# Reordering the first two tiles of a retention-plus-MLP kernel: the second tile's first product ahead of the first tile's second one

## The chip, the cores and the metric

One core of a Trainium2 chip runs the whole program. The metric is the time of one execution on the device in microseconds (us). Engines are named as in the profile: PE is TensorE (PEld its weight loads), DVE is VectorE, ACT is ScalarE, POOL is GpSimd, SP is SyncE, which here issues DMAs only. A line number such as L662 is one of the kernel before, unless it is said to be of the kernel after.

## The reference

```python
def _attn_ref(q, k, v):                      # q, k, v: (8, 8, 576, 64) float32
    scores = np.matmul(q, k.transpose(0, 1, 3, 2)) / np.sqrt(D_)
    gamma = 1.0 - 2.0 ** (-5.0 - np.arange(H))
    rel = pos[:, None] - pos[None, :]
    Dmat = np.where(rel >= 0, gamma[:, None, None] ** rel[None, :, :], 0.0)
    return np.matmul(scores * Dmat[None], v)

def _moe_ref(x, w_in, w_out):                # x: (4608, 512), w_in: (512, 2048), w_out: (2048, 512)
    h = x @ w_in
    g = h * np.tanh(np.log1p(np.exp(h)))     # mish (h itself above 20)
    return g @ w_out
```

The attention's output, with heads side by side, is x. Inputs and output are float32; the kernel multiplies in bf16 and sums in float32.

## The kernel before, in words

**Tiles and chunks.** The 4608 rows of x are worked on as 9 tiles of 512 rows, each of 4 chunks of 128 rows. Tiles 0 and 1 hold the first 128 positions of batches 0 to 3 and 4 to 7; they need no earlier state, and have code of their own (the functions f_*). Chunks 8 to 35 follow: for each, q, k and v are loaded (`load`, by DMAs that POOL issues), multiplied by decay factors (`step_p`, L341, two instructions on DVE; `step_v`, L348, on DVE for chunks below 16, on POOL later), q and k are turned (`step_t`), and then scores (L382), states (L428, summed on DVE at L452), masks (`step_m`, L388) and outputs (L484, L500) follow in a "visit" of two chunks.

**First product of a tile.** `g1(t, f)`: for each of 16 blocks f of d_ff, four products of 128 x 128 weights w_in with 512 columns of x (L570; with `halved` set, the middle ones as two of 256 columns at L575), then Mish on ACT into gT (L586).

**Second product of a tile.** Tile 0: `g2_first`, plain, 4 row blocks x 16 products of 512 columns, with the result copied (L619) and stored. Tiles from 1 on: seven products of halves in place of eight (Strassen-Winograd's kind of scheme): w_out and g are each cut into 2 x 2 quarters; sums of quarters are made ahead (`w_sum`, L643, for w_out, once for all tiles; `g_sum`, L653, for g, five for each tile; each 128 x 2048 bf16), and `unit(t, k)` does half of one of the seven products, 8 matmuls of 256 columns at L662 (`seven`). `taken` moves each finished bank out of PSUM and combines the results; some of the additions are put off (`behind_visit`, `rest`).

**Order.** The scheduler is off: each engine runs its instructions in the order in which the program emits them, and waits on semaphores. The order is written out by hand. In the kernel before: g1(0, 0..15); then the 16 parts of g2_first with tile 1's preparation between them (T: turning, S: scores, V: casts of v, O: outputs, F: states); then the loop over u = 0..23, whose slots 0 to 15 are g1(1, u) and 16 to 23 are unit(1, 0..7), with the work of chunks 8 to 13 between them (`ps`, `vs`, `ts_` say at which u a chunk's P, V and T come). Then tiles from 2 on.

**Loads on POOL's queue.** All loads but the first two go through POOL. Its DMAs use eight semaphores in turn, so that an issue waits until the eighth one before it has landed, and POOL's other instructions stand in the same line. The order before: tile 0's q, k, v; w_in in five pieces; half of tile 1's q and k (L107); w_out 0 and 1 (L89); the other half of q and k; w_out 2 and 3; tile 1's v in two pairs (L118); mask (L935 to L938); chunks 8, 9 and on (L325). Chunks 10 to 17 wait, by a one-column copy on POOL (`landed`, L313), until v of the chunk two before has landed. Five buffers hold q and k of chunks (`qkraw`), seven hold v.

**Banks.** PSUM has the pools sc (2 x 2 banks), st (1), hp (2) and ops (1). Outputs of chunks 8 and 9 take ops and hp at u = 16.

Of the kernel before, what the change touches and what calls it, by code (L numbers as in the profile page):

```python
# [9 lines left out]
F32 = mybir.dt.float32  # L10
# [6 lines left out]
def kernel(  # L17
# [84 lines left out]
    def load_first_qk(t, i, b):  # L102

        name = ("qb", "kb")[i]
        if t not in fst:
            fst[t] = {"qb": stage[:, 0:4, :], "kb": stage[:, 4:8, :], "vb": {}}
        nc.gpsimd.dma_start(out=fst[t][name][:, b, :],  # L107
                            in_=(q, k)[i][4 * t + b, :, 0:P, :].rearrange("h (g r) d -> g h (r d)", r=8))
# [51 lines left out]

    def keep_warm(n, pool=ps_o, name="ops"):
        idle = pool.tile([P, 512], F32, name=name)
        for _ in range(n):
            nc.tensor.matmul(idle, lhsT=zeros[:, 0:P], rhs=zeros, start=True, stop=True)

# [55 lines left out]
    def f_v(t, b, copy):  # L221
# [5 lines left out]
        fst[t]["vb"][b] = vb  # L227

    def f_out(t, b, copy):
        if b == 0:  # L230
            xts[t] = xp.tile([P, KC, NCH * P], BF16, name="xT")
        vb = fst[t]["vb"][b]
        if t == 0:
            pool, name = ((ps_h, "hp"), (ps_h, "hp"), (ps_st, "st"), (ps_o, "ops"))[b]
            ot = pool.tile([P, NP, P], F32, name=name)
        else:
            if b % 2 == 0:
                fst[1]["out"] = ps_sc.tile([P, 2, NP, P], F32, name="sc")
            ot = fst[1]["out"][:, b % 2]
        for p in range(NP):  # L240
            for e in range(2):
                nc.tensor.matmul(ot[ds(64 * e, 64), p, :], lhsT=vb[:, 2 * p + e, :],
                                 rhs=fst[t]["sm", b][:, 2 * p + e, :],
                                 start=(p == 0), stop=True, skip_group_check=True)
        if t == 0:

            n = NP if b < 2 else NP // 2
            for p in range(0, NP, n):
                copy(xts[t][:, ds(p, n), ts(b, P)], ot[:, ds(p, n), :])
        elif b % 2:  # L250
            copy(xts[1].rearrange("p h (b i) -> p b h i", i=P)[:, ds(b - 1, 2)], fst[1]["out"])

# [309 lines left out]

    outs = {}
    halved = [0]
# [23 lines left out]

    def g2_first(part, s):

        if part == 0:
            pool, name = ((ps_h, "hp"), (ps_h, "hp"), (ps_o, "ops"), (ps_st, "st"))[s]
            outs[0, s] = pool.tile([P, d_model], F32, name=name)
        for f in range(4 * part, 4 * part + 4):
            halved[0] = int(f < 9)
            product(outs[0, s], gts[0][:, f, ts(s, P)], w_out_t[:, f, :], f == 0, f == nF - 1)
        if part == 3:
            store(0, s, outs[0, s], nc.scalar.copy if s % 2 else nc.vector.tensor_copy)

# [7 lines left out]
    def send(t, s):  # L607
# [4 lines left out]
        else:  # L612
            for e in range(2):
                nc.sync.dma_start(out=out[ds((b + e) * S + 512, 64), :], in_=ot[ds(64 * e, 64), :])

    def store(t, s, ops, copy):
        if s % 2 == 0:
            rows_of(t, s // 2)
        copy(rows[t, s // 2][:, s % 2, :], ops)  # L619
        send(t, s)  # L620

# [16 lines left out]
    def w_sum(i, engine=nc.vector):  # L638
        a, b, op_, to = {1: ((0, 0), (1, 1), OP.add, room[0]), 6: ((0, 0), (0, 1), OP.add, room[1]),
                         7: ((1, 0), (1, 1), OP.add, room[2]), 3: ((0, 1), (1, 1), OP.subtract, None),  # L640
                         4: ((1, 0), (0, 0), OP.subtract, room[6])}[i]
        to = w_half(*a) if to is None else to.rearrange("p (f d) -> p f d", f=hF)
        engine.tensor_tensor(to, w_half(*a), w_half(*b), op=op_)  # L643
        wsum[i] = to

    def g_sum(t, i, engine=nc.vector, to=None):
        a, b, op_ = {1: ((0, 0), (1, 1), OP.add), 2: ((1, 0), (1, 1), OP.add), 5: ((0, 0), (0, 1), OP.add),
                     6: ((1, 0), (0, 0), OP.subtract), 7: ((1, 1), (0, 1), OP.subtract)}[i]
        if to is None:
            to = room[3 + gsum.setdefault("n", 0) % 3]  # L650
            gsum["n"] += 1
# [25 lines left out]
    def taken(t, i, bank):  # L677

        tt = nc.vector.tensor_tensor
        in_rows = nc.gpsimd.tensor_tensor if t == nT - 2 else tt  # L680
        if i == 4 and t < NS:
            rows_of(t, 1)
            act(quarter(t, 1, 0), bank)
        elif i == 4:
# [4 lines left out]
        elif i == 1:  # L689
            if t >= NS:  # L690
                rows_of(t, 1)
            if (t, 0) not in rows:
                rows_of(t, 0)
            lower = fourth[t] if t >= NS else quarter(t, 1, 0)
            act(keep[1], bank)
# [24 lines left out]

    ORDER = {NS - 1: (4, 3, 2, 1, 6, 5, 7)}
    LIKE = {6: 3, 7: 5}
    banks = {}

    def unit(t, k):

        i, half = ORDER.get(t, (4, 2, 1, 3, 6, 5, 7))[k // 2], k % 2
        if half == 0 and i not in LIKE:
            beside = {4: (ps_h, "hp"), 3: (ps_st, "st")} if t < NS else \
                {2: (ps_st, "st"), 3: (ps_st, "st")} if t == nT - 2 else {}  # L730
# [106 lines left out]
    def tail(t):  # L837
# [21 lines left out]
        act(quarter(t, 0, 1), third)  # L859
        g_sum(t, 6, to=room[6])  # L860
        second = whole(2, ps_h, "hp")
# [35 lines left out]
    for b in range(2):  # L897
        dve(fst[0]["qb"][:, b, :], q0[:, b, :])
    keep_warm(12)
    f_transpose(0, 0, 1, [(ps_h, "hp", act), (ps_h, "hp", dve)])  # L900
    f_transpose(0, 0, 0, [(ps_st, "st", act), (ps_o, "ops", dve)])
    keep_warm(2, ps_sc, "sc")
    f_transpose(0, 1, 1, [(ps_h, "hp", act), (ps_h, "hp", act)])
# [3 lines left out]
    f_v(0, 1, act)  # L907
    load_w_in(1024, 512)
    keep_warm(3, ps_h, "hp")
    f_scores(0, 1)  # L910
    keep_warm(3)
    f_out(0, 0, act)
# [3 lines left out]
    f_v(0, 3, (act, pool))  # L916
    load_w_in(1536, 512)
    f_out(0, 2, act)
    f_out(0, 3, dve)
    keep_warm(2, ps_sc, "sc")  # L920
    f_k0_copy(0, turned, (dve, dve))
    for i, b in ((1, 0), (1, 1), (0, 0), (0, 1)):
        load_first_qk(1, i, b)
    for i in range(2):
        load_w_out(i)
        f_state(0, i)
    for i, b in ((1, 2), (1, 3), (0, 2), (0, 3)):
        load_first_qk(1, i, b)
    for b in (2, 3):
        f_state(0, b)  # L930
    for i in (2, 3):
        load_w_out(i)
    for b in (4, 6):
        load_first_v(b)
    nc.gpsimd.memset(mask, 1.0)  # L935
    for j in range(2):
        half = mask[ds(64 * j, 64)]
        nc.gpsimd.affine_select(out=half, in_=half, compare_op=OP.is_ge, fill=0.0,  # L938
                                base=0, pattern=[[1, 64]], channel_multiplier=-1)
    for b in range(4):  # L940
        load(N0 + b)
    nc.vector.tensor_scalar(gq, gq, 1.0 / math.sqrt(D), None, op0=OP.mult)


    for f in range(nF):
        halved[0] = 2
        g1(0, f)
    for i in range(2):
        f_mix(0, i)
    steps = {0: "T0", 3: "S0 C1", 9: "T1", 11: "S1", 12: "V0 V1 V2 V3", 14: "O0 O1 O2 O3", 15: "F0 F1"}  # L950
    for i in range(nF):
        for step in steps.get(i, "").split():
            n = int(step[1])
            if step[0] == "T":
                for j in range(2):
                    f_transpose(1, n, j, [(ps_sc, "sc", (dve, act)[j])])
            elif step[0] == "S":
                f_scores(1, n)
            elif step[0] == "V":
                f_v(1, n, dve if n == 3 else act)  # L960
            elif step[0] == "C":
                for j in range(2):
                    f_mix(n, j)
            elif step[0] == "F":
                f_state(1, n, nc.vector)
            else:
                f_out(1, n, (dve, act)[n // 2])
        g2_first(i // 4, i % 4)

# [11 lines left out]
    ts_ = {4: 0, 7: 1, 12: 2, 14: 3, 19: 4, 21: 5}  # L981
    FIRST = {1: (0, 0), 2: (1, 0), 3: ("turn", 1), 5: (0, 1), 6: (1, 1)}
    for u in range(24):
        j, w = divmod(u, 4)
        halved[0] = 2 if u < 1 else 0
        if u in FIRST:
            what, of = FIRST[u]
            if what == "turn":
                f_k0_copy(of, f_k0(of), (dve, act))
            else:  # L990
                first_states(of, what)
                if what:
                    first_states_copy(of, act)
        if u in ps:
# [3 lines left out]
        if u in vs:  # L998
            att(N0 + vs[u], "V")
        if u in (1, 2):  # L1000
            f_state(1, u + 1, nc.vector)
        for what in {7: "W4", 9: "W6 W3 W1", 19: "S1", 21: "S6"}.get(u, "").split():
            w_sum(int(what[1])) if what[0] == "W" else g_sum(1, int(what[1]))
        if w == 0 and j > 0:
# [23 lines left out]
        if u < nF:  # L1028
            g1(1, u)
            flush()  # L1030
# [17 lines left out]
    for t in range(NS, nT - 1):  # L1048
        for i in range(nF):
# [8 lines left out]
            if (t, i) in HALVED:  # L1058
                halved[0] = HALVED[t, i]
            for job in PLAN[i] if t > NS else {5: ("S5",), 8: ("W7",), 9: ("S7",)}.get(i, ()):  # L1060
                if job[0] == "S":
# [107 lines left out]
```

## Time and profile before

| | |
|---|---|
| median of 3 runs | 288.64 us (288.28 to 288.77) |
| the profiled execution | 288.53 us |
| its span, first to last instruction | 286.8 us |
| busy: PE, DVE, POOL, ACT | 276.7, 215.5, 172.0, 162.1 us |
| PE busy in 0 to 17 us, 17 to 49 us, 49 to 78 us | 13.28, 31.79, 28.42 us |
| DVE busy in the same stretches | 10.39, 14.50, 28.17 us |
| g1(0, 0) starts, tile 0's second product starts | 16.89 us, 31.67 us |
| g1(1, 0), slot u = 0, starts | 48.90 us |
| unit(1, 6), slot u = 22, starts | 77.20 us |

The page lists busy time by engine, the span in 40 slices, DMA queues, the chain that ended last, and groups of instructions by line. A timeline line has start, duration, engine, line, operation, output <- inputs, size, count, and in brackets how long the engine was idle before it and what ended that. The window table has, for each stretch, its length and the busy time of PE, PEld, DVE, ACT and POOL with numbers of instructions, then the granted PE clock (1.00 throughout), the DMA share and GB/s. The chain is followed back from the end; its lines have start, duration and what it was.

### The profile page before, as it was taken

What the parts mean: (1) busy time and instruction counts of PE and PEld (TensorE: products, weight loads), DVE (VectorE), ACT (ScalarE), POOL (GpSimd) and SP (SyncE); (2) the same over time, 40 slices, a digit from 0 to 9 for tenths busy, and PEclk for the clock granted to TensorE, in tenths of its full rate; (3) what the DMA queues carried; (4) which work ended last, traced back from release to release, by engine and by line L of the source; (5) the groups of instructions that cost most, each with busy time, mean ns of one, the idle gap of its engine ahead of it and who ended that gap; (6) DMA issues with size and microseconds to landing.
All of it is one profiled execution on the core that took longest, in us unless ns stands there. A gap on an engine that the chain in (4) does not pass through costs nothing.

```text
span 286.8 us, 8923 instructions
## 1 busy us (share of the span) xinstructions
PE 276.7 (96%) x3818; PEld 192.9 (67%) x3854; DVE 215.5 (75%) x302; ACT 162.1 (57%) x286; POOL 172.0 (60%) x243
## 2 busy tenths in 40 slices
PE   7799999999999999999999999999999999999994
PEld 3466775556876667666766666667666766888783
DVE  4740459999999996896599757974899194777783
ACT  5566415777776564565465555564566556476620
POOL 8686861687793999697929682969240000469500
PEclk9999999999999999999999999999999999999999
DMA  7999999978799994979599999697968001200323
GB/s 150 205 204 205 204 238 220 305 186 210 190 215 197 166 279 122 210 189 233 145 153 209 141 209 204 167 206 189 154 101 146 2 3 73 75 1 3 108 92 94
DMA packets 41545, 45.94 MB, mean 160 GB/s; under 512 B 23841, under 2 KB 31265, under 8 KB 41505
## 3 DMA queue, kind: packets, MB, share of 16 engines
q0 software_dynamic: 14256, 30.15, 50.1%
q1 hardware_dynamic: 26656, 14.69, 26.4%
q8 instruction: 30, 0.49, 0.8%
q10 hardware_dynamic: 592, 0.52, 0.6%
q14 instruction: 11, 0.08, 0.1%
HBM read 36.70 MB, written 9.44 MB: 161 GB/s over the span
## 4 chain that ended last, share of the span: by engine, by line
PE 69%; DMA 15%; DVE 7%; POOL 5%; issue 2%; ACT 1%; POOLq 0%; ACTq 0%; DVEq 0%
PE hp L570 28%; PE ops L662 27%; DMA w_out_t<-in_moe_w_out_dram 4%; DMA vraw<-in_v_dram 4%; DMA w_in_t<-in_moe_w_in_dram 4%; PE st L662 2%; DMA qkraw<-in_k_dram 2%; PE hp L662 2%; PE hp L778 2%; DVE qks L341 2%; PE sc L778 1%; PE sc L428 1%; PE sc L382 1%; PE sc L849 1%; POOL gT L107 1%
## 5 line engine op out<-in xcount | busy, mean ns | idle before, releaser
L570 PE MATMUL hp<-xT,w_in_t 128*128 128x512 bf16 x439 | 111.8, 379 | 1.8 <-issue 0.3
L586 ACT ACTIVATE gT<-hp 128x512 bf16<-128x512 f32 x129 | 76.9, 600 | 46.6 <-PE hp L570 42.2
L570 PEld LDWEIGHTS <-w_in_t 128*128 128x128 bf16 x474 | 45.3, 98 | 41.0 <-issue 0.9
L662 PEld LDWEIGHTS <-room 128*128 128x128 bf16 x608 | 58.8, 98 | 13.9 <-DVE room L653 0.3
L341 DVE TENSOR_TENSOR qks<-qkraw,gqk 128x512 bf16<-128x512 f32 x56 | 48.1, 908 | 10.1 <-issue 5.1
L653 DVE TENSOR_TENSOR room<-gT 128x2048 bf16<-128x2048 bf16 x40 | 50.8, 1289 | 1.1 <-ACT gT L586 1.1
L1045 POOL COPY held<-gT 128x1 bf16<-128x1 bf16 x58 | 23.0, 397 | 32.9 <-ACT gT L586 32.9
L662 PE MATMUL ops<-room,room 128*128 128x256 bf16 x320 | 40.1, 273 | 0.3 <-DVE room L653 0.2
L796 POOL TENSOR_TENSOR vraw<-vraw 128x256 f32<-128x256 f32 x7 | 6.5, 924 | 37.9 <-ACT vraw L790 37.8
L662 PEld LDWEIGHTS <-gT 128*128 128x128 bf16 x256 | 24.5, 98 | 6.2 <-ACT gT L586 0.4
L388 DVE TENSOR_TENSOR sm<-sc,mask 128x1024 bf16<-128x1024 f32 x14 | 17.1, 1218 | 11.7 <-PE sc L382 11.1
L348 POOL TENSOR_TENSOR vs<-vraw,gv 128x512 bf16<-128x512 f32 x20 | 25.5, 1297 | 0.0
L662 PE MATMUL ops<-w_out_t,room 128*128 128x256 bf16 x208 | 25.3, 273 | 0.0
L325 POOL DMA_DIRECT2D vraw<-in_v_dram x24 | 21.3, 886 | 2.5 <-DMA w_out_t<-in_moe_w_out_dram 1.4
L325 POOL DMA_DIRECT2D qkraw<-in_q_dram x24 | 21.7, 904 | 1.5 <-issue 1.2
L325 POOL DMA_DIRECT2D qkraw<-in_k_dram x24 | 21.2, 884 | 0.0
L452 DVE TENSOR_TENSOR total<-sc,total 128x256 f32<-128x256 f32 x32 | 13.5, 422 | 2.2 <-PE sc L428 1.4
L512 ACT CAST xT<-hp 128x512 bf16<-128x512 f32 x19 | 10.3, 589 | 7.6 <-PE hp L500 7.6
L662 PE MATMUL ops<-room,gT 128*128 128x256 bf16 x112 | 13.7, 272 | 0.2 <-ACT gT L586 0.2
L575 PE MATMUL hp<-xT,w_in_t 128*128 128x256 bf16 x92 | 13.8, 273 | 0.0
L575 PEld LDWEIGHTS <-w_in_t 128*128 128x128 bf16 x92 | 9.0, 98 | 5.4
L175 DVE COPY room<-gT 128x1024 bf16<-128x1024 bf16 x4 | 3.2, 828 | 9.7 <-DMA gT<-in_q_dram 9.7
(186 smaller groups left out, 423.6 us busy)
## 6 DMA issues: line engine op xcount, KB each, us to landing
out_dram<-res SPq DMA_DIRECT2D x29, 256.0 KB, 4.8
qkraw<-in_q_dram POOLq DMA_DIRECT2D x24, 256.0 KB, 6.1
qkraw<-in_k_dram POOLq DMA_DIRECT2D x24, 256.0 KB, 6.4
vraw<-in_v_dram POOLq DMA_DIRECT2D x24, 256.0 KB, 5.4
w_out_t<-in_moe_w_out_dram POOLq DMA_DIRECT2D x4, 512.0 KB, 11.3
w_in_t<-in_moe_w_in_dram POOLq DMA_DIRECT2D x3, 512.0 KB, 10.1
out_dram<-res SPq DMA_DIRECT2D x9, 128.0 KB, 2.4
gT<-in_k_dram POOLq DMA_DIRECT2D x8, 128.0 KB, 6.9
```

The source lines that it names most:

```text
L325: nc.gpsimd.dma_start(out=t, in_=src[b, :, ds(P * c, P), :].rearrange("h p d -> p h d"))
L341: nc.vector.tensor_tensor(slots[:, :, y], heads[:, :, y], factors[:, :, y].unsqueeze(3).to_broadcast([P, NP, 2, D]), op=OP.mult)
L348: engine.tensor_tensor(vs, live[n]["v"], gv[:, c, :].unsqueeze(2).to_broadcast([P, H, D]), op=OP.mult)
L388: nc.vector.tensor_tensor(sm.rearrange("p e x n i -> p (e x n) i"), live[n]["sc"].rearrange("p e x n i -> p (e x n) i"), mask.unsqueeze(1) ...
L452: nc.vector.tensor_tensor(new[:, k], st[:, j, x], total[b], op=OP.add)
L512: copy(xts[t][:, :, ds(P * s, 2 * P)].rearrange("p h (x j i) -> p j h x i", x=2, j=2)[:, j], both[j])
L570: nc.tensor.matmul(to, lhsT=w, rhs=x, start=first, stop=last)
L575: nc.tensor.matmul(to[:, ts(j, n)], lhsT=w, rhs=x[:, ts(j, n)], start=False, stop=False, skip_group_check=True)
L586: nc.scalar.activation(gts[t][:, f, :], hp, AX.Mish)
L653: engine.tensor_tensor(to, g_half(t, *a), g_half(t, *b), op=op_)
L662: nc.tensor.matmul(bank[:, half, :], lhsT=g[:, f, ts(half, P)], rhs=w[:, f, :], start=(f == 0 and half == 0 and not add), stop=(f == hF - ...
L1045: nc.gpsimd.tensor_copy(held[:, i % 2:i % 2 + 1], gts[t][:, f, 0:1])
```

## The change

1. After g1(0, f), which now has tile 1's first turning, scores and outputs (batches 4 and 5) between its last blocks, comes tile 1's first product, by halves of its batches: `g1_half(i, 0)` for batches 4 and 5, then `g1_half(i, 1)` for 6 and 7, each for two blocks of d_ff, 8 matmuls of 256 columns and one Mish. x of tile 1 is laid out as two halves (`x1`), and each half is copied by ACT and DVE together.
2. Tile 0's second product comes after that, by seven products of halves as in the other tiles, `unit(0, u - 2)` in the slots u = 2 to 15 that held g1(1, u). Its order is 5, 2, 7, 4, 3, 1, 6, and `taken_first` takes its banks. Its g sums 5 and 7 go to two of the five qkraw buffers (`ahead`); sums 2, 1 and 6 to room as in other tiles. `g2_first` and `store` are gone.
3. w_out's sums are all made ahead of tile 0's second product: 4, 6, 3 and 1 on DVE, and 7 on POOL. In the kernel before all are on DVE, 4, 6, 3 and 1 between u = 7 and 9, and 7 in tile 2.
4. Loads: half of tile 1's q and k goes ahead of the last three (smaller) pieces of w_in, then v, q and k of tile 1, and w_out last: pieces 2 and 3, then 0 and 1. Tile 1's q and k go to two of the buffers for output rows (`res`).
5. `f_state(0, b)` goes from POOL to DVE, `f_state(1, b)` from DVE to POOL, and tile 1's four casts of v go from ACT (three) and DVE (one) to POOL. w_sum 7 and the mask stand on POOL behind chunks 8 and 9's loads and ahead of chunk 10's.
6. The warming products on PE are cut into more and smaller ones.

Its core, with other parts left out:

```diff
@@ load_first_qk
-        if t not in fst:
-            fst[t] = {"qb": stage[:, 0:4, :], "kb": stage[:, 4:8, :], "vb": {}}
+        if t == 0 and t not in fst:
+            fst[0] = {"qb": stage[:, 0:4, :], "kb": stage[:, 4:8, :], "vb": {}}
+        elif t not in fst:
+            held_ = [op.tile([P, 2, d_model], F32, name="res").rearrange("p x d -> p (x d)").bitcast(BF16)
+                     for _ in range(2)]
...
@@ g2_first
+    def g1_half(i, j):
+
+        if 1 not in gts:
+            gts[1] = gp.tile([P, nF, NCH * P], BF16, name="gT")
+        hp = ps_h.tile([P, 2, 2 * P], F32, name="hp")
+        for a in range(2):
+            for c in range(KC):
+                nc.tensor.matmul(hp[:, a], lhsT=w_in_t[:, c, ts(2 * i + a, P)], rhs=x1[j][:, c, :],
+                                 start=(a == 0 and c == 0), stop=(c == KC - 1), skip_group_check=True)
+        nc.scalar.activation(gts[1][:, ds(2 * i, 2), ds(2 * P * j, 2 * P)], hp, AX.Mish)
...
+    def taken_first(i, bank):
+
+        tt, in_rows = nc.vector.tensor_tensor, nc.gpsimd.tensor_tensor
+        if i == 5:
+            rows_of(0, 0)
+            act(quarter(0, 0, 1), bank)
+        elif i == 2:
+            act(keep[0], bank)
+        elif i == 7:
+            act(quarter(0, 0, 0), bank)
+        elif i == 4:
+            lower = op.tile([P, 2, hD], F32, name="fourth", bufs=1)
+            act(lower, bank)
+            rows_of(0, 1)
+            behind_visit.append(lambda: in_rows(quarter(0, 0, 0), lower, quarter(0, 0, 0), op=OP.subtract))
+            behind_visit.append(lambda: in_rows(quarter(0, 1, 0), lower, keep[0], op=OP.add))
+        elif i == 3:
+            tt(quarter(0, 0, 1), bank, quarter(0, 0, 1), op=OP.add)
+        elif i == 1:
+            tt(quarter(0, 0, 0), bank, quarter(0, 0, 0), op=OP.add)
+            tt(quarter(0, 1, 1), bank, keep[0], op=OP.subtract)
+        else:
+            tt(quarter(0, 1, 1), bank, quarter(0, 1, 1), op=OP.add)
+
+    ORDER = {0: (5, 2, 7, 4, 3, 1, 6), NS - 1: (4, 3, 2, 1, 6, 5, 7)}
...
@@ the order, from the first loads on
-    keep_warm(12)
+    keep_warm(50, cols=122)
...
-    load_w_in(1024, 512)
-    keep_warm(3, ps_h, "hp")
+    load_w_in(1024, 256)
+    keep_warm(8, ps_h, "hp", 192)
...
-    load_w_in(1536, 512)
+    for i, b in ((1, 0), (1, 1), (0, 0), (0, 1)):
+        load_first_qk(1, i, b)
...
-    for i in range(2):
-        load_w_out(i)
-        f_state(0, i)
+    for f0 in (1280, 1536, 1792):
+        load_w_in(f0, 256)
+    load_first_v(4)
     for i, b in ((1, 2), (1, 3), (0, 2), (0, 3)):
         load_first_qk(1, i, b)
-    for b in (2, 3):
-        f_state(0, b)
+    load_first_v(6)
     for i in (2, 3):
         load_w_out(i)
...
     for b in range(4):
-        load(N0 + b)
+        f_state(0, b, nc.vector)
...
+    for i in (1, 0):
+        f_mix(0, i)
     for f in range(nF):
+        if f == 11:
+            for i in (1, 0):
+                f_transpose(1, 0, i, [(ps_sc, "sc", dve)])
+        elif f == 13:
+            f_scores(1, 0)
+        elif f == 14:
+            first_states(0, 0)
+            for b in range(2):
+                f_v(1, b, pool)
+            for i in (0, 1):
+                load_w_out(i)
+        elif f == 15:
+            for b in range(2):
+                f_out(1, b, (act, dve))
         halved[0] = 2
         g1(0, f)
...
+    def ahead(i, to=None):
+        g_sum(0, i, to=io.tile([P, 2, H, D], F32, name="qkraw").rearrange("p i h d -> p (i h d)").bitcast(BF16))
+
+    for i in range(8):
+        if i == 1:
+            for m in (1, 0):
+                f_mix(1, m)
+            ahead(5)
+            first_states_copy(0, act)
+        elif i == 2:
+            f_transpose(1, 1, 1, [(ps_sc, "sc", dve)])
+            f_transpose(1, 1, 0, [(ps_sc, "sc", act)])
+            for b in (2, 3):
+                f_v(1, b, pool)
+            for b in range(4):
+                f_state(1, b)
+            for b in range(2):
+                load(N0 + b)
+            w_sum(7, nc.gpsimd)
+            nc.gpsimd.memset(mask, 1.0)
...
+            load(N0 + 2)
+            ahead(7)
+            load(N0 + 3)
+        elif i == 4:
+            f_scores(1, 1)
+        elif i == 7:
+            for b in (2, 3):
+                f_out(1, b, (act, dve))
+        g1_half(i, 0)
+    for i in range(8):
+        if i == 1:
+            f_k0_copy(1, f_k0(1), (act, act))
+            g_sum(0, 2)
+        elif i == 3:
+            first_states(1, 0)
+        elif i == 5:
+            first_states(1, 1)
+            first_states_copy(1, act)
+            for m in (4, 6, 3):
+                w_sum(m)
+        g1_half(i, 1)
...
-    for u in range(24):
+    att(N0, "P")
+    att(N0, "V")
+    w_sum(1)
+    for u in range(2, 24):
...
-        for what in {7: "W4", 9: "W6 W3 W1", 19: "S1", 21: "S6"}.get(u, "").split():
-            w_sum(int(what[1])) if what[0] == "W" else g_sum(1, int(what[1]))
+        if u in (5, 9, 19, 21):
+            g_sum(int(u > nF), 1 if u in (5, 19) else 6)
+        if u == 11:
+            rest()
+        for s in {14: (0, 1), 17: (2, 3)}.get(u, ()):
+            send(0, s)
...
         if u < nF:
-            g1(1, u)
+            unit(0, u - 2)
             flush()
```

## The prediction

> **What bounds the kernel now.** I read the page's busy shares and its 40 slices first, then busy time by stage, then the chain in order of time, then the timelines of VectorE (DVE), GpSimd (POOL) and TensorE (PE) for the first 110 us.
>
> ```profile
> PE 276.7 (96%) x3818; PEld 192.9 (67%) x3854; DVE 215.5 (75%) x302; ACT 162.1 (57%) x286; POOL 172.0 (60%) x243
> ...
> 17.00:49.00 32.00, 31.79 (x285) 22.15 (x288) 14.50 (x19) 14.93 (x23) 19.08 (x26) 1.00 1.18 215
> 49.00:78.00 29.00, 28.42 (x630) 19.12 (x633) 28.17 (x42) 22.66 (x41) 22.51 (x31) 1.00 0.87 223
> ```
>
> PE is busy 96% of the span, so work taken off PE looks like time gained. The second fence line is 17 to 49 us (PE, PEld, DVE, ACT, POOL busy), where DVE has 17 us free; the third is 49 to 78 us, where DVE is busy 28.17 of 29.00 us, as much as PE. The two are in balance there, and the chain goes through DMA and DVE, not through PE:
>
> ```profile
> 36.91 12.21 DMA vraw<-in_v_dram
> 49.73 0.88 POOL qkraw L325
> 50.61 6.68 DMA qkraw<-in_k_dram
> 57.39 1.29 DVE qks L341 x2
> ...
> 76.00 1.15 DVE room L653
> 77.20 1.92 PE ops L662 x16
> ```
>
> Read it as: attention chunk 10's k was issued at 50.61 and landed at 57.3; DVE took it up at 57.39 and then worked without a pause worth naming until 77.15, the sum g_sum(1, 1); PE's product with that sum waited for it:
>
> ```profile
> 77.20 1.92 PE L662 MATMUL ops<-room,room 128*128 128x256 bf16 x16 [0.23 <-DVE room L653]
> ```
>
> So this DVE list has no more than about 0.2 us of slack at its end. What comes after 77.2 us is not changed, so **the change is worth what it does to the moment at which PE gets through this product** (slot u = 22).
>
> **Part 1, PE's work.** From the chain, eight 512-column products take 1.73 us and eight 256-column ones 0.87. Tile 0's second product: 64 x 512 columns, 8 x 1.73 = 13.84 us; by seven products of halves 14 units x 0.87 = 12.18. That is -1.66. Tile 1's first product goes to halves: 16 x 0.87 = 13.92 for 13.84, +0.08. Sum -1.6 us. The warming products keep their columns (22 x 512 = 11,264 against 11,236), and stand beside the first loads: nothing.
>
> **Part 2, the loads.** They are one queue on POOL, and from 24 to 44 us it moves a steady 205 GB/s. The same bytes (w_in, tile 1's q, k, v, w_out) go in another order, so the last of them, now w_out's, lands when before's last (v, issued 33.29, 12.2 to landing) did: 45.5 us. w_in's columns from 1280 on come behind four of tile 1's loads: by bytes they land at 25.3, where PE comes to them at 25.6 (16.9 + 10 x 0.87); 0 to 0.3 us, and, like other short PE waits up to 45 us (two scores and an output product behind DVE's copies and masks, about 1 us by my walk), no cost as long as DVE's list decides later. Splitting x into halves and ACT's Mish over 2 x 256 keeps 16 of 0.60 us each. Tile 0's four products with gv go from POOL to DVE: 4 x 0.6 us at 18 us, beside a DVE pause of 9.66 us. The stores of tile 0 leave SP's queue at 46 to 50 us and go at u = 14 and 17; 1 MB among loads, at 4.8 us to landing: nothing on the path, up to 0.5.
>
> **Part 3, DVE's list from 45.5 us.** Its first three items, w_sum 4, 6, 3, read all of w_out, so they start when that lands. Up to chunk 10's product with the factors (L341): three w_sums 3 x 1.14 = 3.4; chunk 8 (L341 x2 and L348) 1.8; w_sum 1 1.14; chunk 9 1.8; g_sum(0, 1) 1.13. That is 9.3 us: 54.8. In before it starts at 57.39. From there to the end of g_sum(1, 1): before 19.66 us (57.39 to 77.05). After: three w_sums go (-3.4), tile 0's g_sum 6 (+1.13) and four additions from PSUM (4 x 0.6 = +2.4) come: 19.8. By DVE alone PE's slot would be reached at 74.6, sooner than PE's own 75.6: DVE would cost nothing and -1.6 would be the result.
>
> **Part 4, what stands in the way: w_sum 7 on POOL.** No 2048-column sum on POOL is in the trace. Two f32 sums on POOL are: 256 columns 0.73, 512 columns 1.27, so 0.54 for each further 256, and 0.73 + 7 x 0.54 = 4.5 us. Bounds: by the casts (0.40 and 0.61) 1.9; by eight times 0.73, 5.8. I take 4.5, the rows of the same operation. What it does to DVE, the trace shows in both directions:
>
> ```profile
> 61.89 0.96 POOL L313 COPY landed<-vraw 128x1 f32<-128x1 f32 x1
> ...
> 61.60 1.22 DVE L643 TENSOR_TENSOR room<-w_out_t 128x2048 bf16<-128x2048 bf16 x1
> ...
> 136.66 2.49 POOL L348 TENSOR_TENSOR vs<-vraw,gv 128x512 bf16<-128x512 f32 x2
> ...
> 136.84 2.85 DVE L341 TENSOR_TENSOR qks<-qkraw,gqk 128x512 bf16<-128x512 f32 x2 [1.62 <-issue]
> ```
>
> POOL's one-column copy takes 0.18 us alone; here it takes 0.96 and ends at 62.85, with DVE's sum (62.82). And DVE's pair of L341, 1.29 alone, takes 2.85 beside two of POOL: whoever comes second waits for the whole instruction, and they alternate. So DVE is held for all of w_sum 7: between 0 (no hold) and 5.8; I take 4.5. The Trainium skill, page "SBUF — State Buffer", section "SBUF: two separate sides", says that the port pair is a lock held for a whole instruction, against DVE operations with two SBUF inputs. By that rule DVE's sums and factor products are all held, and its PSUM copies not; without the rule the term would be 0, with it the 4.5 of the rows.
>
> When does POOL come to it? Tile 1's second v pair lands at 35.4; two casts behind a DVE sum until 37.8; four f_state at 1.05 with one DVE sum between, 43.1 (40.9 if nothing holds any of them); six issues for chunks 8 and 9 at 0.88, 48.4. Then w_sum 7, behind w_sum 3: 48.9 to 53.4. So DVE reaches chunk 10 at 54.8 + 4.5 + 0.5 (two selects for the mask) = **59.8**.
>
> And chunk 10's loads are queued on POOL behind w_sum 7, the mask and a copy that waits for chunk 8's v. Before: issued at 49.7. After: 53.4 + 0.2 memset + 1.5 (two selects of 0.24, each behind half of a L341 pair) + 0.3 = 55.4; k one issue later, 56.3. To landing: 6.7 us for this load in before, with others queued ahead, 4.4 for chunk 12's with none: 60.7 to 63.0, near the lower, since the queue has run empty. So the load is the later of the two: DVE takes chunk 10 up at **60.7**, 3.3 us after before. Chunks 11 and 12 now wait for the buffers of chunks 8 and 9, two being lent to tile 0's sums; by the same issues they land 1 to 3 us ahead of need.
>
> **The sum.** 60.7 + 19.8 = 80.5; the first addition from bank ops waits for a POOL addition queued behind chunk 13's loads and contends with it: +0.5, 81.0, against 77.05 before: **+4.0 us**. PE loses its 1.6 us and waits in all some 5.6 us more, in pieces: transposes of chunks 8 to 11, and longest ahead of the output products of chunk 8 (bank ops still held by DVE's additions). Profiled execution of before: 288.53 us (span 286.8 and 1.7 around it); median 288.64, 0.1 apart. 288.5 + 4.0 = **292.5 us**.
>
> **Rivals.**
> A, faster: w_sum 7 runs beside DVE without holding it and is over early (the casts' rate, 1.9 us). Then chunk 10 is taken up at 54.8 and PE's -1.6 stays: 286.9. Each us by which DVE takes chunk 10 up earlier than 57 is gained, down to 55.4, where PE's own work decides. For it: POOL could go first while DVE waits for w_out, as w_sum 7 needs only the half of w_out that lands at 40.5. Against: POOL has twelve instructions ahead of it, and the two rows above. 0.13.
> B, smaller loss: w_sum 7 at 2 to 3 us, or POOL some 2 us earlier at it: chunk 10 at 58 to 59.3, 289.2 to 290.8. 0.15.
> Forecast, 290.8 to 294.6: 0.57.
> C, worse: PE's waits are long enough to slow it. The 12 warming products at the start take 4.28 us, 0.36 each against 0.216 later, so a cold start costs 12 x 0.14 = 1.7 us; with one or two of those, or with w_sum 7 at 5.8 and the load at 6.7, 294.6 to 298. Against: my longest single wait is 2 to 3 us. 0.10. The Trainium skill, page "TensorE: Matmul & The Clock Gate", section "Part 1: The HAM clock gate", puts the slow clock after an idle window of about 3.4 us; by that rule C needs a longer wait than mine.
> D, gain and loss cancel: 288.1 to 289.2: 0.05.
>
> A run of this kernel can tell about 0.2% (0.6 us) from no change. Faster 0.13, same 0.05, slower 0.82. The range from 289.0 to 296.0 leaves out A, most of D and the end of C, some 0.2, and takes in both bounds of the load; the lower bounds of w_sum 7 are B and A.
>
> **What would show it.** In after's timelines: one POOL sum of about 4.5 us near 49 to 53, a DVE operation of two SBUF inputs stretched by as much beside it; chunk 10's k issued near 56, DVE's L352 on it near 61; the slot's product near 81; PE idle in 49 to 82 up from 0.6 to about 6 us, PE busy in all 1.6 us less. Wrong if POOL reaches w_sum 7 before 45.5, if DVE goes on beside it, or if chunk 10 lands before 57.

## The result and the profile after

The kernel after takes 297.97 us (median of 5 runs, 297.33 to 298.34), the one before 288.64: ratio 1.0326, interval 1.0310 to 1.0342, so +9.3 us. The forecast was slower, +4.0. Some executions of a kernel take some per cent longer than its others; the times and ratios below leave them out, and of e2, e5 and e9, whose profiled execution was or may have been such a one, mainly neighbouring durations are read. Line numbers from here on are those of the kernel after; in e7 they are one higher.

The first lines of its page, and the window table of the same stretches as for before (columns as there):

```profile
PE 282.6 (95%) x3988; PEld 207.5 (70%) x3988; DVE 229.8 (77%) x308; ACT 162.1 (55%) x286; POOL 188.1 (63%) x252
```

```profile
17.00:49.00 32.00, 31.07 (x396) 23.33 (x394) 22.74 (x25) 20.21 (x35) 25.82 (x31) 1.00 1.17 210
49.00:78.00 29.00, 23.68 (x344) 19.33 (x344) 27.64 (x30) 11.03 (x21) 28.13 (x29) 0.90 0.60 144
78.00:88.00 10.00, 9.34 (x283) 8.33 (x275) 9.93 (x16) 6.20 (x11) 6.22 (x10) 0.96 0.91 259
```

From 49 to 78 us PE falls from 28.42 to 23.68 us of work, and at a clock of 0.90. DVE is shown busy for nearly all of it (27.64 us), yet it has 30 instructions there where before it had 42: **an engine that is held counts as busy**. The chain in order of time (start, duration, what) gives the place. It calls the hold "issue":

```profile
44.05 0.47 issue
44.52 0.70 DVE room L657
45.22 7.74 issue
52.95 2.44 DVE room L647 x2
...
56.55 1.30 DVE qks L352 x2
...
68.29 0.13 DVE qks L352
68.42 1.45 issue
69.87 0.75 DVE qks L352
70.62 1.99 issue
72.61 1.21 DVE sm L399
```

And the product of slot u = 22, in PE's timeline, at 77.20 before:

```profile
87.31 1.92 PE L666 MATMUL ops<-room,room 128*128 128x256 bf16 x16
```

That is +10.1 us, and the span is +9.8 (286.8 to 296.6). From this product to the end it is 209.3 us, before 209.6: the loss lies ahead of it, as the prediction assumed. DVE's timeline of after, with the operations that took longer than alone or waited:

```profile
44.52 8.51 DVE L657 TENSOR_TENSOR room<-gT 128x2048 bf16<-128x2048 bf16 x1
...
62.44 1.28 DVE L352 TENSOR_TENSOR qks<-qkraw,gqk 128x512 bf16<-128x512 f32 x2
...
66.57 0.42 DVE L463 TENSOR_TENSOR total<-sc,s 128x256 f32<-128x256 f32 x1 [1.11 <-PE sc L439]
...
68.29 4.39 DVE L352 TENSOR_TENSOR qks<-qkraw,gqk 128x512 bf16<-128x512 f32 x2
```

The first, a sum of gate rows, takes 1.22 us alone: held 7.3 us. The second is chunk 10, taken up at 62.44 and not at 60.7. The last, chunk 11's pair, takes 1.28 alone: held 3.1 us. POOL's timeline beside them:

```profile
46.96 0.89 POOL L336 DMA_DIRECT2D vraw<-in_v_dram  x1
47.86 4.08 POOL L647 TENSOR_TENSOR room<-w_out_t 128x2048 bf16<-128x2048 bf16 x1
...
56.27 0.88 POOL L336 DMA_DIRECT2D qkraw<-in_k_dram  x1
...
69.95 0.88 POOL L336 DMA_DIRECT2D vraw<-in_v_dram  x1
70.85 1.28 POOL L737 TENSOR_TENSOR res<-fourth,res 128x512 f32<-128x512 f32 x1
72.07 1.74 POOL L738 TENSOR_TENSOR res<-fourth,dmask 128x512 f32<-128x512 f32 x1
```

w_sum 7 starts at 47.86, but DVE's sum of 44.52 stands already; the row additions start at 70.85, but chunk 11's pair stands from 68.4 (its first instruction is held 0.97 us, its second 2.13). Both POOL sums come straight behind DMA issues, and **DVE is held while POOL still shows the issues.**

### The profile page after: what moved, and what is told of

Same layout as the page of the kernel before. It is cut to its first block, busy times and chain, and to the rows that moved or that the text cites. A ratio compares the mean times of both kernels' runs of the same rounds, so it can differ in the third digit from the quotient of the medians.

```text
span 296.6 us, 9250 instructions
## 1 busy us (share of the span) xinstructions
PE 282.6 (95%) x3988; PEld 207.5 (70%) x3988; DVE 229.8 (77%) x308; ACT 162.1 (55%) x286; POOL 188.1 (63%) x252
## 4 chain that ended last, share of the span: by engine, by line
PE 78%; issue 6%; DVE 5%; DMA 5%; ACT 2%; POOL 2%; POOLq 0%; SPq 0%; ACTq 0%; DVEq 0%
PE hp L580 29%; PE ops L666 27%; PE st L666 3%; PE hp L585 3%; DMA gT<-in_v_dram 3%; PE hp L666 2%; DMA out_dram<-res 2%; PE hp L606 2%; PE hp L805 2%; PE sc L439 1%; PE sc L393 1%; PE sc L805 1%; PE sc L876 1%; POOL gT L112 1%; DVE room L647 1%
## 5 line engine op out<-in xcount | busy, mean ns | idle before, releaser
L580 PE MATMUL hp<-xT,w_in_t 128*128 128x512 bf16 x408 | 99.9, 379 | 0.1
L596 ACT ACTIVATE gT<-hp 128x512 bf16<-128x512 f32 x113 | 67.1, 598 | 46.1 <-PE hp L580 45.2
L666 PEld LDWEIGHTS <-room 128*128 128x128 bf16 x656 | 64.5, 100 | 16.4 <-issue 1.2
L580 PEld LDWEIGHTS <-w_in_t 128*128 128x128 bf16 x412 | 39.9, 98 | 35.4 <-issue 0.2
L657 DVE TENSOR_TENSOR room<-gT 128x2048 bf16<-128x2048 bf16 x43 | 60.8, 1430 | 1.1 <-ACT gT L596 1.1
L352 DVE TENSOR_TENSOR qks<-qkraw,gqk 128x512 bf16<-128x512 f32 x56 | 49.7, 935 | 7.8 <-issue 4.4
L666 PE MATMUL ops<-room,room 128*128 128x256 bf16 x336 | 42.0, 273 | 0.0
L666 PEld LDWEIGHTS <-gT 128*128 128x128 bf16 x288 | 27.6, 98 | 6.6 <-ACT gT L596 0.4
L666 PE MATMUL ops<-w_out_t,room 128*128 128x256 bf16 x224 | 28.9, 283 | 0.0
L606 PE MATMUL hp<-xT,w_in_t 128*128 128x256 bf16 x128 | 15.4, 273 | 0.5 <-DVE xT L262 0.4
L606 PEld LDWEIGHTS <-w_in_t 128*128 128x128 bf16 x128 | 12.2, 98 | 2.4 <-issue 0.6
L585 PE MATMUL hp<-xT,w_in_t 128*128 128x256 bf16 x88 | 13.2, 272 | 0.0
```

The lines of the kernel that those rows point to most:

```text
L352: nc.vector.tensor_tensor(slots[:, :, y], heads[:, :, y], factors[:, :, y].unsqueeze(3).to_broadcast([P, NP, 2, D]), op=OP.mult)
L580: nc.tensor.matmul(to, lhsT=w, rhs=x, start=first, stop=last)
L585: nc.tensor.matmul(to[:, ts(j, n)], lhsT=w, rhs=x[:, ts(j, n)], start=False, stop=False, skip_group_check=True)
L596: nc.scalar.activation(gts[t][:, f, :], hp, AX.Mish)
L606: nc.tensor.matmul(hp[:, a], lhsT=w_in_t[:, c, ts(2 * i + a, P)], rhs=x1[j][:, c, :], start=(a == 0 and c == 0), stop=(c == KC - 1), skip_ ...
L657: engine.tensor_tensor(to, g_half(t, *a), g_half(t, *b), op=op_)
```

## The experiments

Theory T1: a POOL sum with nothing left to wait for takes the port that it shares with DVE while it still stands behind issues. T2: the issues take the port. T3: only the sum's own shown run does. e1, e2, e3, e7 and e9 test these; e4, e6, e8, e11 and e5 ask where the rest of the time went.

**e1**, w_sum 7 back on DVE:

```diff
-            w_sum(7, nc.gpsimd)
...
-            for m in (4, 6, 3):
+            for m in (7, 4, 6, 3):
```

> The changed kernel with w_out's sum 7 on DVE (first of the list 7, 4, 6, 3) and nothing in its place on POOL. Theory 1 (a POOL instruction that reads SBUF and has no wait left takes the shared port as soon as it stands in the queue, behind the DMA issues ahead of it, and keeps it until it has run): g_sum 2 at 44.5 us takes 1.2 us and not 8.5, the list starts when w_out has landed (45.6), chunk 10's q and k are issued 4 us sooner (near 51), DVE takes them up near 57.5; the hold of 3 us at chunk 11 stays. Slot 22 near 80, total 289.5 to 292. Theory 2 (the DMA issues themselves hold the port against DVE operations with two SBUF inputs): g_sum 2 still takes some 4.5 us, to the end of the issues at 47.9; total 291 to 293. Theory 3 (the prediction's: only the sum's own 4.1 us hold DVE, the rest of the 8.5 us is a wait that the trace does not show): g_sum 2 keeps some 4 us.

Measured: 292.69 us, ratio to before 1.0148 (1.0124 to 1.0172), 5.3 us less than after; clock 1.00 throughout. DVE's timeline:

```profile
45.01 1.22 DVE L657 TENSOR_TENSOR room<-gT 128x2048 bf16<-128x2048 bf16 x1
46.14 3.49 DVE L647 TENSOR_TENSOR room<-w_out_t 128x2048 bf16<-128x2048 bf16 x3
...
56.74 1.28 DVE L352 TENSOR_TENSOR qks<-qkraw,gqk 128x512 bf16<-128x512 f32 x2
...
63.27 0.42 DVE L463 TENSOR_TENSOR total<-sc,s 128x256 f32<-128x256 f32 x1 [3.51 <-PE sc L439]
```

The six issues are nearly where they were (43.05 to 48.4 us, in after 42.5 to 47.9), and nothing beside them is held: T2 falls. Chunk 10 comes 5.7 us earlier, but DVE then waits 3.51 us for PE's states, where in after it waits 1.11: it now runs ahead of PE, at a place of its list where it needs PE, and loses 2.4 of the 5.7 us again. Chunk 11's pair takes 2.95 us, so it is held 1.7 us and not the 3 that were expected to stay. Slot u = 22 starts at 82.04, later than the 80 expected, and the time is just above the range given.

**e2**, w_sum 7 on POOL, behind a one-column copy that waits for chunk 8's v:

```diff
+            (a copy of one column of chunk 8's v, as in `landed`)
             w_sum(7, nc.gpsimd)
```

> The changed kernel with one more one-column copy on POOL just ahead of w_sum 7, which waits until chunk 8's v has landed (near 50 us). The sum stays on POOL. Theory 1: the sum cannot be queued before that wait is over, so g_sum 2 at 44.5 us takes 1.2 us, and a DVE operation is held later, once the sum is let through, for about 4 us. Theory 2: g_sum 2 is held to the end of the DMA issues (47.9), 3 to 4.5 us. Theory 3: g_sum 2 takes 4 to 5 us less than now or stays as it is. Total by theory 1: 295 to 299, since chunk 10's loads come later still by 2 to 3 us.

Measured: 296.47 us, ratio 1.0275 (1.0251 to 1.0298). DVE's sums beside the six issues (POOL 44.49 to 49.8) are as short as alone, and one DVE operation beside the sum's run (POOL 51.86 to 56.37) is held:

```profile
46.51 1.22 DVE L657 TENSOR_TENSOR room<-gT 128x2048 bf16<-128x2048 bf16 x1
...
52.37 4.55 DVE L359 TENSOR_TENSOR vs<-vraw,gv 128x512 bf16<-128x512 f32 x1
```

4.55 less 0.68 is 3.9 us: one hold, not 7.3. The early hold needs a sum that waits for nothing.

**e3**, e1 and, in w_sum 7's old place on POOL, a sum of one column:

> w_sum 7 on DVE as in e1_w7_dve, and in its place on POOL a sum of one column of two constants (128 x 1, long ready, no wait). Theory 1: it takes the port as early as w_sum 7 did, so g_sum 2 at 44.5 us lasts until the six DMA issues and this sum are over, near 48: 3.5 us in place of 1.2 in e1_w7_dve; total 1 to 2.5 us above e1_w7_dve. Theory 2: g_sum 2 as in e1_w7_dve, whatever that is, and the same total within 0.3. Theory 3: g_sum 2 takes 1.2 us, the same total within 0.3.

Measured: 293.38 us (292.28 to 295.16), ratio 1.0179 (1.0124 to 1.0235). The sum of gate rows is not held, so not every POOL sum does it; whether its size decides, e7 asks:

```profile
44.47 1.22 DVE L657 TENSOR_TENSOR room<-gT 128x2048 bf16<-128x2048 bf16 x1
```

**e7_pool512 and e7_pool64**, the same with 512 and 64 columns:

```diff
-            w_sum(7, nc.gpsimd)
+            nc.gpsimd.tensor_tensor(junk[:, 0:512], w_in_t[:, 0, 0:512], w_in_t[:, 1, 0:512], op=OP.add)
```

> The eighth sum of w_out's blocks is on VectorE, and in its old place behind GpSimd's six transfer issues stands a sum of 512 bf16 columns into a tile that nobody reads (1 column was not enough to hold VectorE). Theory (a large GpSimd sum claims the shared port while it is still queued behind the issues, as soon as its operands are there): the second sum of gate rows, which starts at about 44.5 us, is held to the end of the small sum at about 48.9 us, so it takes about 4.4 us. Rival (the port is claimed only while the sum runs, 47.9 to 48.9 us): the sum of gate rows takes 1.2 us, and a later sum of VectorE's list is lengthened by at most 1 us. Rival (only a sum as large as 2048 columns does it): 1.2 us and no later lengthening.

> The same with 64 columns. If the claim comes with the first operand read ahead, whatever the size, VectorE is held as with 512 columns (about 4 us). If it comes because the reads of a large sum can not all be done ahead of its run, 64 columns lie between: no hold (1.2 us) if they fit, 4 us if not.

Measured: 296.20 and 293.34 us (one run each). With 512 columns, DVE:

```profile
44.32 1.22 DVE L658 TENSOR_TENSOR room<-gT 128x2048 bf16<-128x2048 bf16 x1
45.45 2.17 DVE L648 TENSOR_TENSOR room<-w_out_t 128x2048 bf16<-128x2048 bf16 x1
...
48.68 2.17 DVE L648 TENSOR_TENSOR room<-w_out_t 128x2048 bf16<-128x2048 bf16 x1
```

and with 64:

```profile
44.22 1.34 DVE L658 TENSOR_TENSOR room<-gT 128x2048 bf16<-128x2048 bf16 x1
...
47.75 1.32 DVE L648 TENSOR_TENSOR room<-w_out_t 128x2048 bf16<-128x2048 bf16 x1
```

POOL shows the sums at 47.87 to 49.76 and 47.62 to 47.98. The hold of 4.4 us from 44.5 on that T1 gave is not there. Instead DVE is held **twice**: 0.95 us ahead of the shown run and 0.95 in it with 512 columns, 0.12 and 0.11 with 64; the DVE operation between is not held. That is 1.7 to 1.9 ns a column each time. For 2048 columns two holds would make 7.0 to 7.7 us, and after has 7.3 in one piece, in which the two can't be told apart. T1 becomes T1': a sum behind issues takes the port once while they are still being made, and again in its shown run. The totals say little here: with 512 columns the slot starts at 81.00, with 64 at 81.72, and the longer time comes from what follows the slot (213.5 us to the end, against 209.9).

**e9**, w_sum 7 on POOL, but ahead of the six issues:

```diff
+            w_sum(7, nc.gpsimd)
             for b in range(2):
                 load(N0 + b)
-            w_sum(7, nc.gpsimd)
```

> The eighth sum stays on GpSimd, but ahead of the six transfer issues of chunks 8 and 9, not behind them (its half of w_out has landed by then). So far, the sum behind the issues held VectorE for 7.3 us, about twice its own run of 4.1 us; a sum of 512 columns in the same place held it twice, 0.95 us each time, for a sum that takes 0.95 us; behind a copy that waits, it held VectorE once, 3.9 us. Theory (the doubling comes with the place behind issues, where the sum begins while they are still being made): ahead of them GpSimd shows it at about 42.5 to 46.6 us, and VectorE's second sum of gate rows, from 44.5 us, is held once and to the end of that run only, so it takes about 3.2 us. Rival (such a sum always takes the port twice): it is held to about 50 us and takes 5.5 us or more. The time is 292 to 297 us either way, since chunks 8 and 9 are issued 4 us later.

Measured (one run): POOL shows the sum at 44.79 to 48.84, and DVE:

```profile
46.80 3.13 DVE L657 TENSOR_TENSOR room<-gT 128x2048 bf16<-128x2048 bf16 x1
49.85 2.35 DVE L647 TENSOR_TENSOR room<-w_out_t 128x2048 bf16<-128x2048 bf16 x2
```

Held to the end of that run and not again, as T1' said. The time, 306.7 us, was 10 us over what was expected, with a mean clock of 0.978. That excess lies behind the slot (219.0 us from there to the end, in after 209.3); where it came from was not pursued.

**e4**, the two row additions of L737 and L738 on DVE, w_sum 7 still on POOL:

```diff
-        tt, in_rows = nc.vector.tensor_tensor, nc.gpsimd.tensor_tensor
+        tt = in_rows = nc.vector.tensor_tensor
```

> The changed kernel with the two additions into tile 0's rows (behind chunk 13's loads on POOL) on DVE; w_sum 7 stays on POOL. Theory 1: chunk 11's pair of factor products, 4.4 us now beside three DMA issues and the first of these additions, takes 1.3; DVE has two additions more, 1.3 us; slot 22 1.5 to 2.5 us sooner, total 295 to 296.5. Theory 2: the pair still waits for the three issues, some 2.5 to 3 us; total 297 to 298. Theory 3: the pair loses only the addition's own 1.3 us, to 3.1; total 297 to 298.

Measured: 295.69 us, ratio 1.0269 (1.0214 to 1.0324), 2.3 us less than after; one of the four runs took 298.34, as long as after. Chunk 11's pair is as short as alone again, and the slot starts at 83.41, 3.9 us earlier, more than the 1.5 to 2.5 expected:

```profile
67.14 1.28 DVE L352 TENSOR_TENSOR qks<-qkraw,gqk 128x512 bf16<-128x512 f32 x2
...
83.41 1.92 PE L666 MATMUL ops<-room,room 128*128 128x256 bf16 x16 [0.43 <-DVE room L657]
```

Not all of the 3.9 us is the additions': the clock is 1.00 here, and the wait of 1.11 us for PE's states is gone too. The first hold stays (the sum of gate rows takes 8.56 us).

**e6**, e1 and e4 together:

> The eighth sum and the two row additions all on VectorE, so that GpSimd makes no large sum of two tiles beside VectorE's list in this stage. Theory (the two holds are what was mis-sized): no operation of VectorE between 44 and 88 us is longer than alone, and the time is the 292.7 us of the eighth sum alone, less the 1.7 us that the pair of chunk 11 is still held there, plus up to 1.2 us for the two additions: 291 to 292.5 us. Rival (the two repairs add up in full, 5.0 and 2.3 us): 290.5 us. Rival (VectorE's waits for TensorE's states swallow the second): 292.7 us.

Measured: 292.14 us, ratio 1.0110 (1.0045 to 1.0175). No operation of DVE between 44 and 80 us takes longer than alone, the clock is 1.00, and the slot starts at 80.70. The two repairs do not add up: the wait for PE's states, 3.23 us here, takes part of both.

**e8**, e1 with that wait filled: the last chunk's products at u = 10, ahead of the sums of states, and the casts of states on ACT:

```diff
-    ps = {0: 0, 4: 1, 8: 2, 11: 3}
-    vs = {0: 0, 5: 1, 9: 2, 13: 3, 18: 4, 19: 5}
+    ps = {0: 0, 4: 1, 8: 2, 10: 3}
+    vs = {0: 0, 5: 1, 9: 2, 10: 3, 18: 4, 19: 5}
...
-            run(casts, dve if u == 13 else act)
+            run(casts, act)
```

> The eighth sum is on VectorE; the products with decay factors and v of the last chunk go to VectorE ahead of the sums of states of the chunk before, not behind them, and the casts of states go to ScalarE. Theory (VectorE's list alone sets the slot in which the second sum of the gate's rows of batch 1 is taken up, by its own length and by the place where it waits for TensorE's states): the wait of 3.5 us for the states in the run with the eighth sum on VectorE is filled with the last chunk's products, that slot comes at 77 to 79 us and the time at 287.5 to 290 us. Rival (TensorE's own queue up to that slot is the bound once the port is free): slot at 80 to 82 us, time 291 to 293 us.

Measured: 293.29 us (290.75 to 293.73), ratio 1.0128 (1.0090 to 1.0167). The slot came where it was expected, the time did not:

```profile
78.76 1.92 PE L666 MATMUL ops<-room,room 128*128 128x256 bf16 x16 [0.42 <-DVE room L657]
```

```profile
99.68 1.29 DVE L352 TENSOR_TENSOR qks<-qkraw,gqk 128x512 bf16<-128x512 f32 x2 [3.12 <-DMA qkraw<-in_k_dram]
```

20 us later a chunk's k lands late, 12.03 us after its issue, PE waits, and its clock falls to 0.50 for about 3 us. The row additions, on POOL at 65.78 and 67.01, hold nobody here: the DVE operations beside them read PSUM.

**e11**, e8 with e4:

> The kernel with VectorE's shorter list (eighth sum on VectorE, the last chunk's products ahead of the sums of states, casts on ScalarE) and the two row additions on VectorE as well. If GpSimd's additions still delay the loads behind them (chunk 16's k landed 3.1 us late there), the time falls by 1 to 2 us, to 290 to 291.5 us; if not, the slot comes 0 to 1 us later and the time is 293 to 294 us.

Measured: 289.91 us (10 runs, 289.23 to 291.58), ratio to before 1.0034 (1.0004 to 1.0065), 8.1 us less than after. The slot starts at 79.73, the late landing is gone, the clock is 1.00. Why it is gone is open: POOL issues that k at 87.37, in e8 at 87.56.

**e5**, nine products of 512 columns that nobody reads on PE ahead of the turnings at u = 4 and 14:

> Products whose result nobody reads (nine of 512 columns, about 2 us) are put on TensorE ahead of the copies of transposed k and q of chunks 10 and 11, where TensorE waits for VectorE. Theory (the two stretches at half clock come from TensorE's waits there and cost their share of the end): the granted clock stays at 1.0 between 54 and 82 us, and the time falls by 1 to 2 us against the changed kernel, to 296 to 297 us. Rival (the slow clock is hidden behind VectorE's list, which sets the end alone): clock 1.0 and the same time within 0.5 us. Rival (the dips don't depend on these waits): they stay, and the time rises by up to 2 us.

Measured: 298.99 us (298.58 to 301.65), ratio 1.0377 (1.0328 to 1.0427): not faster than after, whose interval (1.0310 to 1.0342) overlaps this one. In the profiled execution the two stretches at half clock are gone, but there is a new one behind a wait of 2.20 us. What the slow clock costs by itself this run does not tell.

## Why the prediction was wrong

**The step that failed is part 4, "DVE is held for all of w_sum 7: between 0 (no hold) and 5.8; I take 4.5".** POOL's side was near: 4.08 us at 47.86 (4.5 at 48.9). That chunk 10's k was issued at 56.27 (56.3) is luck: the sum was over 1.5 us sooner than forecast, and the mask and the copy behind it took 1.4 us more. The mechanism was right: the hold is w_sum 7's (e1). Its size was not: 7.3 us, since a sum behind issues holds DVE a second time, ahead of its run (e7 shows the two holds apart; ahead of the issues, e9, and behind a wait, e2, there is one). The bound of 5.8 was worked out from durations of runs, which do not contain that. So DVE itself came to chunk 10 at 62.44, and not the load, which had landed by then, decided. That is 1.7 of the 6.3 us between 81.0 and 87.31. The Trainium skill, "SBUF — State Buffer", section "SBUF: two separate sides", states the lock, and by it the hold is one instruction long; the measured 7.3 us beside a run of 4.08 decides. A sentence of its page "GPSIMD Engine Reference", section "4. When to use GPSIMD", fits two holds: a DMA's descriptors are made by a pair of POOL's cores. If the other cores take up a sum that stands behind the issues, and the pair only afterwards, the port is taken twice. No trace here shows the cores, so this is not shown.

**The second miss, and the larger one at the slot, is in the sum: "contends with it: +0.5"** for the row additions. It is the same step: a hold priced too low. The 0.5 was for DVE's first addition from bank ops; that the additions hold chunk 11's pair, some 8 us ahead of it in DVE's list, was not in the sum. They held it for 3.1 us, some 1.9 of it ahead of their run (in e4 the pair takes 1.28 us). That is 2.6 us more than forecast.

**Rival C** (0.10) has a range, 294.6 to 298, that takes in the result; but by another way: the hold was past even C's 5.8, since it comes twice, and the load did not decide. C's other cause, a slower PE, is there too. Its condition was dismissed wrongly: "a longer wait than mine" was not needed. PE's timeline of after:

```profile
57.90 0.70 PE L373 MATMUL sc<-ident,qks 128*128 128x128 bf16 x8 [1.96 <-DVE qks L352]
58.39 3.53 PE L666 MATMUL ops<-w_out_t,room 128*128 128x256 bf16 x16
...
72.74 0.62 PE L373 MATMUL sc<-ident,qks 128*128 128x128 bf16 x8 [2.19 <-DVE qks L352]
74.47 2.74 PE L666 MATMUL hp<-room,room 128*128 128x256 bf16 x16 [1.11 <-DVE res L740]
```

Sixteen products that take 1.92 us took 3.53, behind a wait of 1.96 us; from 58 to 62 and from 75 to 79 us the clock is 0.57. The second stretch comes behind two waits close together, 2.19 and 1.11 us. In e4 a wait of 2.01 us at the place of the first left the clock at 1.00, and so did one of 2.03 us later. The rule cited, slow after an idle window of about 3.4 us (the Trainium skill, "TensorE: Matmul & The Clock Gate", section "Part 1: The HAM clock gate"), does not hold here as a lower limit for one wait. The cost, as far as shown, is DVE's wait of 1.11 us for PE's late states, which e4, at full clock, does not have. With 0.66 us that PE waits for a copy by ACT ahead of the slot, and 0.2 in small ones, the 6.3 us are complete: 1.7 + 2.6 + 1.1 + 0.7 + 0.2. The first two of these rest on e1 and e4, the other three are read from the trace of after alone.

**Part 1** gave PE -1.66 us of work. From the first product of tile 0 to the slot PE is busy 59.05 us in e8 and 59.60 in e11, before 59.52: at most 0.5 less. Where the rest of the gain went was not found. **Part 2** held for w_out (in e1 the first sum of it starts at 46.14 without a wait), but not for "no cost as long as DVE's list decides later": once it does not, PE's small waits count (in that stretch 1.9 us in e11, 0.8 before). The first product starts at 18.22 us in e11 (16.89 before), which is 1.3 of the 2.5 us by which its slot is later than before. In after, e1, e3, e4, e6, e7 and e8, with the same order of loads, it lies between 16.95 and 17.82 us, so whether that order moves it is open. **Part 3**, the length of DVE's list without holds, was right to 0.2 us: in e1 it takes 10.6 us from 46.14 to chunk 10 at 56.74, by the sum 9.3 and w_sum 7's 1.1. What it left out is a wait in the list behind chunk 10: without the hold DVE stands 3.51 us for PE's states. **Rival A** is refuted in its condition, and its time was too low besides: e6, in which no operation of DVE is held in this stage, is still 3.2 us slower than before. With e8's order of DVE's list 2.2 of these are gone (e11).

## What to carry to other kernels

A POOL operation on two SBUF tiles is not free beside a DVE list of such operations, or of casts: price it at its run, and at twice its run where it follows DMA issues on POOL's queue with nothing left to wait for, and look for the hold in DVE operations that are longer than alone, not in idle time. Where an engine is freed by some microseconds, read the next place in its list at which it needs another engine; here that place took back 2.4 of 5.7 us. A reordering that fills both PE and DVE leaves no slack for waits that cost nothing before.

## What the runs showed of the hardware that was not expected

- A POOL sum behind issues holds DVE twice: 2 x 0.12 us for 64 columns, 2 x 0.95 for 512, 7.3 in all for 2048 (run 4.08). Behind a wait 3.9, ahead of the issues once. For one column nothing was seen.
- Not only sums and products of two tiles are held. In e7_pool512 a cast on DVE with one SBUF input, 0.69 to 0.86 us where no POOL addition ran beside it, took 1.75 us beside POOL's second row addition:

```profile
67.88 1.73 POOL L739 TENSOR_TENSOR res<-fourth,dmask 128x512 f32<-128x512 f32 x1
...
68.41 1.75 DVE L471 CAST ssb<-total 128x1024 bf16<-128x1024 f32 x1
```

- The two engines need not alternate. A one-column copy on POOL in after took 3.78 us (0.18 to 0.2 alone); five DVE instructions, one of them under way at its start, ran in that time, against the "they alternate" of the prediction:

```profile
61.73 3.78 POOL L324 COPY landed<-vraw 128x1 f32<-128x1 f32 x1 [0.67 <-DMA vraw<-in_v_dram]
```

- PE's clock was halved for about 3.4 us behind a wait of 1.96 us, and again behind waits of 2.19 and 1.11 us close together, but not behind single waits of 2.01 (e4) and 2.10 us (e7_pool512).
